# Landmark sums of two batches by DMA transfers that add, negated row maxima in tiles of their own, and a new order of work (Nyström attention, then a squared-ReLU MLP, one core)

## The chip, the cores and the metric

The kernel runs on one core of one Trainium2 chip. The metric is the device time in microseconds (us) of one execution, as a median of several runs. One further execution was recorded by the hardware profiler; every duration below comes from its trace, and line numbers such as L486 are lines of the kernel before. In the changed file the same statements stand some 3 to 34 lines further down.

The engines are PE (TensorE, matrix products), DVE (VectorE), ACT (ScalarE), POOL (GpSimd) and SP (SyncE). Each works through its own instructions in program order and waits at an instruction whose inputs are not there. Loads are issued by POOL, stores by SP (the very last one by ACT too).

## The reference, cut to what matters

```
q, k, v: (8 batches, 8 heads, 576 tokens, 64) float32;   m = 32 landmarks, 18 tokens each
q_lm = mean of q over each run of 18 tokens;   k_lm likewise
A  = softmax(q  k_lm^T / 8)        (576 x 32)
Bm = softmax(q_lm k_lm^T / 8)      (32 x 32)
C  = softmax(q_lm k^T / 8)         (32 x 576)
Z  = Bm^T / (norm1(Bm) * norminf(Bm) + 1e-6);   6 times: Z = 2 Z - Z Bm Z
x  = A Z C v, heads side by side:  (4608 tokens, 512)
out = relu(x w_in)^2 w_out,        w_in 512 x 2048, w_out 2048 x 512
```

## The kernel before

All work is cut into named steps, some 1400 of them. Batch b (0 to 7) is one round of `attention(b)`, `ffn1(b)` and pieces of `ffn2`. A table `ORDER` lists the steps in one line of words; the position of a word sets the order in which its engine meets it, and a suffix (`/A`, `/D`, `/P`, `@bank`) sets the engine or the PSUM bank. So the order on every engine's queue is written out by hand (or by a search); a small planner only checks it against its own costs and fills gaps of the first 30 us with idle products on `onesb` (L1198).

The steps that matter here:

- `ldq`, `ldk`, `ldv` (L425, L441): POOL issues the load of q, k or v of half a batch, float32 in memory to bfloat16 on the chip. 288 KB arrive per transfer of q or k; for v there are transfers of 288, 216 and 72 KB.
- `lx` (L431) and `lm` (L486), batches 3 to 7: `lx` loads q and k of the batch a second time, laid out by runs of tokens in the tile `XS` (96 partitions); `lm` sums the 18 tokens of each landmark with 48 products on PE, and `lme` (L414 or L418) copies the scaled sums from PSUM into `LM`. `lmt` transposes them (L544), and `B`, `SS` (L560, L743, L748) need the result. Batches 0 to 2 sum with the identity in other forms (L501, L508).
- `N`, `U`, `bd`: the six iterations for Z. `bd` (L649) spreads a 32 x 32 block to a diagonal tile `BD`, on POOL or on DVE; the product `N` on PE (L712) needs it; `U` (L726, DVE) makes the next iterate.
- `Amx`, `Aex`, `Asu`, `Arc`, `Aml` of batches 0 and 1: the softmax of A. In batch 0, cut in four parts (`BY_ROW`), `Amx` (L973, DVE) writes the negated row maxima into the tile `smA`, and `Aex` (L978) is one ACT instruction per row with that maximum as its bias.
- `CV` (L834), `ZC`, `W` (L905, into PSUM, copied to `WP` by `We`), `F` (L1077, the first MLP product, into PSUM), `R` and `Q` (ReLU and square on ACT or DVE), `O` (L1124, the second MLP product; one step is four products of a 128-token tile), `Oe` and `St` (copy and store of a 128-token tile, 256 KB).

Of the kernel before, what the change touches and what calls it, by code (L numbers as in the profile page):

```python
# [264 lines left out]
def kernel(  # L265
# [32 lines left out]
    XS = mk("XS", [96, 2, H, 6, D], BF16)  # L298
# [21 lines left out]
    smA = [mk(f"smA{u}", [P, 3, 2, n], F32) for u, n in enumerate(A_LEN)]  # L320
    w_in = mk("w_in", [P, 4, D_FF], BF16)
# [106 lines left out]
    def load_xs(b):  # L428
        for t in range(2):
            src = (q, k)[t][b].rearrange("h (p j) d -> p h (j d)", j=6)  # L430
            op(f"lx{b}.{t}", {"POOL": 0.8}, lambda e, t=t, src=src: nc.gpsimd.dma_start(  # L431
                XS[:, t].rearrange("p h j d -> p h (j d)"), src),
               W=[("XS", t)], nbytes=1179648, queue="sw")

# [25 lines left out]
    def attention(b):  # L460
# [17 lines left out]
        def landmarks_rows():  # L478
# [3 lines left out]
            def lmx(e):  # L482
                xs = XS[:].rearrange("p t (r c) j d -> p t r c j d", r=2)
                for j in range(6):
                    for c in range(4):
                        nc.tensor.matmul(view()[quad(c)], lhsT=seg[:], rhs=xs[:, :, :, c, j, :],  # L486
                                         start=(j == 0), stop=(j == 5))
# [450 lines left out]
        for u in range(2) if b in TOKENS else ():  # L938
# [28 lines left out]
            for j, (x0, x1) in enumerate(zip(cuts, cuts[1:])):  # L967
# [4 lines left out]
                op(f"Amx{b}.{u}{z}", {"DVE": v_(w)}, lambda e, s3=s3, p3_=p3_, pS=pS, at=at, neg=by_row:  # L972
                   nc.vector.tensor_reduce(s3(0)[:, at], p3_(pS)[:, at], axis=AX.X, op=ALU.max, negate=neg),  # L973
                   R=[pS], W=kx_("amx"))

                def rows(e, s3=s3, sa3=sa3, p3_=p3_, pS=pS, x0=x0, x1=x1):
                    for x in range(x0, x1):
                        nc.scalar.activation(sa3[:, x], p3_(pS)[:, x], AF.Exp, bias=s3(0)[:, x:x + 1])  # L978
# [8 lines left out]
                op(f"Asu{b}.{u}{z}", {"DVE": v_(w)}, lambda e, s3=s3, sa3=sa3, at=at: eng(e).tensor_reduce(  # L987
# [172 lines left out]
    def loads(what, b):  # L1160
# [53 lines left out]
ROWS = (3, 4, 5, 6, 7)  # L1214
# [14 lines left out]
ROW = 0.12  # L1229
# [31 lines left out]
R1.4 St2 F1.12@5 R1.0 N2.3@2 Q1.4 lm3.0@7 U2.3 R1.12 Q1.0 bd2.4/D F1.8@2 lme3.0 Q1.12 lx4.0
N2.4@5 F1.14@0 lmt3.0 R1.8 U2.4 ldk5.1 Q1.2 B3@6 R1.14 F1.20@4 Bmx3 Bsb3 T3.01 ldv2.00 Bex3 R1.20
SS2.0@0,2,6 Bsu3 At2.0 Q1.20/A ldv3.10 SS2.1@4 Q1.14/A bd2.5 Cmx2.0 O5.0@6 lx4.1 Cmx2.1 Cex2.0
O5.1 At2.1 Cex2.1 F1.22@0 Brc3 Amx2.0 Bml3/P F1.10@4 ldq6.1 R1.22 Btf3 F1.28@2 Crc2.1 Asb2.0
R1.10 O4.0@7 ldk4.0 Q1.22 R1.28 ldv3.11 Amx2.1 N2.5@5 F1.16@0 Btr3/A Q1.8/A Bcs3 U2.5 F1.18@2
Zm2.0 R1.16 Zm2.1 Bct3 F1.30@4 Zm2.3 Bnm3 Aex2.0 bt3/D O4.1 Q1.10 Asb2.1 R1.18 O4.2 ldv4.11
Cnr2.1 R1.30 Bad3 Brn3 Asu2.0 Q1.18/A Zi3/P F1.24@2 F1.26@4 T3.00 Aex2.1 O4.3 Q1.16 R1.26 ldq6.0
CT2.1 R1.24 BBT3@0 O5.2 Yi3 Arc2.0 Asu2.1 bd3.0 Q1.24/A O5.3 ldq5.0 Oe4.0 Aml2.0 ldv3.00 Q1.26/A
SS3.0@2,4,0 St4 O7.0@7 Q1.28/A At3.0 Oe5.0 O7.1 Ab2.0 St5 Crc2.0 Arc2.1 Cnr2.0/A Aml2.1 SS3.1@0
O6.0@6 Q1.30/A Cmx3.1 O6.1 At3.1 Cex3.1 CT2.0 O7.2 Cmx3.0 Amx3.0 CV2@4,0 Cex3.0 Crc3.1 Zm2.2 O7.3  # L1270
CVe2.0/A CVe2.1 ldv5.11 T4.11 ldv5.00 ZC2@3 N3.0@5 O6.2 Asb3.0 ZCe2.0 ldk6.0 ZCe2.1 ldv4.00 U3.0
W2.1@2 Aex3.0 Amx3.1 W2.2@0 W2.0@4 bd3.1 Oe7.0 Ab2.1 O6.3 We2.0/D We2.1 St7 O8.0@7 We2.2 Crc3.0
# [6 lines left out]
lm5.0@5 Q2.9/A Zm3.0 CV3@2,0 Btf4 R2.13 Zm3.2 Q2.12 O9.1 Btr4/A lme5.0/D CVe3.0/A ldv6.10 Zm3.1
Q2.14/A Arc3.1 Aml3.1 lx6.1 O10.0@5 CVe3.1/A Ab3.1 lx6.0 ZC3@6 O10.1 lmt5.0 ZCe3.0 Bcs4 Ab3.0  # L1280
ZCe3.1 ldv5.10 Q2.13/A Bct4 B5@2 W3.0@6 bt4 Bnm4 Q2.15/A Bmx5 W3.1@0 Bad4 Bsb5 O10.2 ldk5.0
We3.1/D Bex5 We3.0 O10.3 Bsu5 Brc5 T4.00 BBT4@6 F3.0@0 Bml5/P Oe10.0 ldv6.00 F3.1@2 Btf5 Brn4
R3.0 St10 Zi4 O9.2 Yi4 R3.1 bd4.0/D T4.10 N4.0@7 Q3.1/A W3.3@5 U4.0 W3.2@0 F3.2@2 We3.3 bd4.1
We3.2/D O12.0@7 R3.2 Q3.0 F3.5@5 Btr5/A Q3.2 N4.1@2 F3.6@0 T5.00 R3.5 O9.3 R3.6 Bcs5 Bct5 Q3.5
F3.7@5 Oe9.0 U4.1 F3.3@0 bd4.2/D St9 F3.4@2 R3.3 N4.2@4 O12.1 R3.4 U4.2 bd4.3/D Q3.6/A Bnm5
F3.10@0 T5.11 N4.3@4 Q3.3/A F3.9@2 U4.3 O12.2 bd4.4/D R3.9 R3.10/D R3.7 N4.4@4 O12.3 U4.4 bd4.5/D
Q3.9 F3.13@2 Oe12.0 Q3.10 N4.5@6 O11.0@5 Bad5 R3.13 bt5/D U4.5 Zm4.3 BBT5@0 Q3.13/A Brn5
SS4.0@1,3,6 Yi5 Q3.4/A bd5.0/D O11.1 Zi5 Zm4.0 Zm4.2 c7 At4.0 Q3.7/A N5.0@0 O11.2 Amx4.0 SS4.1@6
U5.0 O11.3 Cmx4.0 bd5.1 Cmx4.1 O13.0@0 Oe11.0 At4.1 Cex4.1 O13.1 St11 Cex4.0 N5.1@5 F3.11@6 U5.1
St12 Asb4.0 F3.8@3 R3.11 O14.0@5 R3.8/D Q3.11/A F3.14@6 Crc4.1 Aex4.0 Amx4.1 F3.12@1 Cnr4.1  # L1290
# [78 lines left out]
```

## Time and profile before

| | |
|---|---|
| median of 3 runs | 261.68 us (261.16 to 262.84) |
| the profiled execution | 261.07 us, of which the span from first to last instruction is 259.4 us |
| PE busy | 249.6 us, 96% of the span |
| DVE, ACT, POOL busy | 210.0, 181.1, 67.9 us |
| idle products on PE (L1198) | 44, in the first 30 us |
| read from memory, written | 48.50 MB, 9.44 MB |

An engine's busy time is an average over very different stages. What matters is, stage by stage, which engine never rests and what it waited for when it did.

### The profile page before, as it was taken

The numbers are of one execution on the slowest core, as the hardware profiler recorded it, in microseconds if no ns is written. First come the engines' busy times: TensorE is split into PE (matmuls) and PEld (weight loads), VectorE is DVE, ScalarE is ACT, GpSimd is POOL, SyncE is SP. The second block draws the span as 40 slices with busy tenths as digits, with TensorE's granted clock in tenths as the row PEclk, the third lists the DMA queues.
The fourth block names the chain that finished last, engine by engine and source line by source line (L and its number), as shares of the span: only waits on it lengthen the run. The fifth ranks groups of instructions, "written<-read, shape, count | busy, mean of one in ns | idle before, by whom it ended". The sixth has DMA issues, their size and how long they took to land.

```text
span 259.4 us, 7586 instructions
## 1 busy us (share of the span) xinstructions
PE 249.6 (96%) x3094; PEld 139.6 (54%) x3094; DVE 210.0 (81%) x547; ACT 181.1 (70%) x362; POOL 67.9 (26%) x117
## 2 busy tenths in 40 slices
PE   7987999999999998999999999999999999999993
PEld 2555565556554566465454556466454575457542
DVE  3678997788999999897999789989899999757321
ACT  4576797578998889788687498886693994367300
POOL 8555827434731540620231411000002000000000
PEclk9999999999999999999999999999999999999999
DMA  6999999999999999794259595051103050033034
GB/s 107 203 189 204 205 212 206 208 238 230 223 208 222 223 217 226 108 211 118 48 95 167 103 204 104 4 124 40 43 3 81 3 123 3 3 87 77 13 91 101
DMA packets 25123, 34.18 MB, mean 132 GB/s; under 512 B 2432, under 2 KB 14464, under 8 KB 25088
## 3 DMA queue, kind: packets, MB, share of 16 engines
q0 software_dynamic: 19168, 24.25, 55.2%
q1 hardware_dynamic: 5760, 9.31, 13.9%
q8 instruction: 24, 0.39, 0.6%
q10 hardware_dynamic: 160, 0.13, 0.2%
q14 instruction: 11, 0.09, 0.1%
HBM read 48.50 MB, written 9.44 MB: 223 GB/s over the span
## 4 chain that ended last, share of the span: by engine, by line
PE 73%; DMA 12%; POOL 5%; issue 4%; ACT 3%; DVE 1%; POOLq 0%
PE ps L1124 42%; PE ps L1077 19%; DMA XS<-in_k_dram 9%; DMA X<-in_q_dram 3%; PE ps L905 3%; ACT SA L978 2%; PE ps L834 2%; POOL X L425 1%; PE ps L486 1%; PE ps L748 1%; POOL V L441 1%; PE ps L1003 1%; POOL BD L649 1%; PE ps L1198 1%; PE ps L712 1%
## 5 line engine op out<-in xcount | busy, mean ns | idle before, releaser
L1124 PE MATMUL ps<-w_out,G 128*128 128x512 bf16 (+1 forms) x592 | 138.0, 374 | 0.0
L1124 PEld LDWEIGHTS <-G 128*128 128x128 bf16 x592 | 54.2, 98 | 54.4 <-issue 5.7
L1098 ACT ACTIVATE RS<-ps 128x576 bf16<-128x576 f32 (+2 forms) x106 | 64.9, 652 | 14.2 <-PE ps L1077 7.0
L1077 PE MATMUL ps<-AT,WP 128*128 128x288 bf16 (+2 forms) x512 | 72.2, 286 | 0.1
L1077 PEld LDWEIGHTS <-WP 128*128 128x128 bf16 x512 | 47.9, 98 | 20.0 <-issue 2.9
L1105 ACT ACTIVATE G<-RS 128x576 bf16<-128x576 bf16 (+2 forms) x50 | 33.5, 687 | 1.7 <-DVE RS L1100 1.2
L1107 DVE TENSOR_TENSOR G<-RS 128x576 bf16<-128x576 bf16 (+2 forms) x76 | 32.4, 447 | 2.2 <-ACT RS L1098 1.6
L412 ACT COPY OS<-ps 128x512 f32<-128x512 f32 (+1 forms) x31 | 17.7, 572 | 21.7 <-PE ps L1124 20.9
L649 POOL TENSOR_TENSOR BD<-ST,blkb 128x256 bf16<-128x256 bf16 x13 | 9.8, 751 | 61.1 <-DVE ST L726 61.0
L412 ACT CAST WP<-ps 128x1024 bf16<-128x1024 f32 (+1 forms) x23 | 21.6, 981 | 3.9 <-PE ps L905 3.7
L470 DVE STREAM_TRANSPOSE TT<-X 128x576 uint32<-128x576 uint32 x32 | 23.8, 758 | 0.1
L789 ACT ACTIVATE C<-ps,sm 128x576 bf16<-128x576 f32 x16 | 14.2, 904 | 10.7 <-DVE sm L786 10.6
L441 POOL DMA_DIRECT2D V<-in_v_dram x24 | 12.8, 534 | 30.6 <-PE ps L834 22.8
L1100 DVE TENSOR_SCALAR RS<-ps 128x576 bf16<-128x576 f32 (+2 forms) x22 | 16.4, 752 | 4.5 <-PE ps L1077 3.8
L726 DVE SCALAR_TENSOR_TENSOR ST<-ST,ps 128x128 bf16<-128x128 bf16 (+1 forms) x48 | 12.6, 263 | 5.2 <-PE ps L712 2.0
L1198 PE MATMUL ps<-onesb 128*128 128x512 bf16 (+1 forms) x41 | 12.5, 413 | 1.6 <-DVE onesb L348 1.6
L416 DVE CAST WP<-ps 128x1024 bf16<-128x1024 f32 (+1 forms) x11 | 12.3, 1114 | 0.9 <-PE ps L905 0.7
L786 DVE TENSOR_REDUCE sm<-ps 128x1 f32<-128x576 f32 x16 | 11.5, 742 | 0.9 <-PE ps L748 0.9
L416 DVE COPY OS<-ps 128x512 f32<-128x512 f32 x6 | 4.1, 688 | 10.1 <-PE ps L1124 10.0
L1030 DVE STREAM_TRANSPOSE SA<-ps 128x320 f32<-128x320 f32 (+1 forms) x24 | 10.0, 455 | 0.5 <-PE ps L743 0.5
L905 PE MATMUL ps<-w_in,ZC 64*32 64x512 bf16 x256 | 10.2, 382 | 0.0
L425 POOL DMA_DIRECT2D X<-in_k_dram x16 | 9.3, 582 | 2.5 <-DMA w_out<-in_moe_w_out_dram 1.0
(142 smaller groups left out, 291.6 us busy)
## 6 DMA issues: line engine op xcount, KB each, us to landing
out_dram<-OS SPq DMA_DIRECT2D x70, 128.0 KB, 2.4
X<-in_k_dram POOLq DMA_DIRECT2D x16, 288.0 KB, 9.3
X<-in_q_dram POOLq DMA_DIRECT2D x16, 288.0 KB, 11.4
XS<-in_q_dram POOLq DMA_DIRECT2D x5, 576.0 KB, 9.0
XS<-in_k_dram POOLq DMA_DIRECT2D x5, 576.0 KB, 12.1
V<-in_v_dram POOLq DMA_DIRECT2D x8, 288.0 KB, 9.4
w_in<-in_moe_w_in_dram POOLq DMA_DIRECT2D x8, 256.0 KB, 10.4
w_out<-in_moe_w_out_dram POOLq DMA_DIRECT2D x4, 512.0 KB, 11.1
```

Of the source, the lines that this page charges most:

```text
L412: nc.scalar.copy(o, i)
L416: eng(e).tensor_copy(o, i)
L441: lambda e, r=r, p0=p0, n=n, src=src: nc.gpsimd.dma_start(vv[32 * p0:32 * (p0 + n), r].rearrange("p s d -> p (s d)"), src),
L470: op(f"T{b}.{t}{r}", {"DVE": v_(576) + 0.02}, lambda e, r=r: nc.vector.transpose(tt[:, t, r].rearrange("p s m e -> p (s m e)").bitcast(U32 ...
L905: nc.tensor.matmul(ps[quad(pos_a(c, r)), pW.at + r, :], lhsT=zcs[r][half, pos_c(c, r), :], rhs=w_in[half, c, 512 * ch:512 * ch + 512], sta ...
L1077: nc.tensor.matmul(ps[:, ph.at + i, 0:w], lhsT=wp[:, r, 128 * ff:128 * ff + 128], rhs=at[:, r, t0:t0 + w], start=(r == 0), stop=(r == 1))
L1098: nc.scalar.activation(rs, pair(ph, w), AF.Relu)
L1100: nc.vector.tensor_scalar(out=rs, in0=pair(ph, w), scalar1=0.0, scalar2=None, op0=ALU.max)
L1105: nc.scalar.activation(g, rs, AF.Square)
L1107: eng(e).tensor_tensor(g, rs, rs, ALU.mult)
L1124: nc.tensor.matmul(bank(po)[:, 0:c1 - c0], lhsT=G[:, f, lo:lo + P], rhs=w_out[:, f, c0:c1], start=(f == 0), stop=(f == NF - 1))
L1198: nc.tensor.matmul(ps[:, j, 0:w], lhsT=onesb[:, 0:P], rhs=x[:, 0:w], start=True, stop=True)
```

## The change

Three things change.

First, batches 6 and 7 no longer use `lx` and `lm`. Instead `load_sums` has POOL issue 18 transfers per batch (`la`), nine for q and nine for k. Each brings two of the 18 tokens of every landmark: 128 partitions, each with 2 runs of 128 float32 numbers, 128 KB. The first of nine writes, the other eight add to what lies there, so each must wait until the one before it has landed; POOL does the waiting. The sums lie as float32 in the space of `XS` (batch 6 in its q half, batch 7 in its k half). What is left are two places per landmark, which `lmc` (ACT) and `lme` (DVE) scale and add into `LM`. PE has no part in it.

Second, in batch 0 the negated maxima of the four parts go to four small tiles `NM` instead of `smA`.

Third, `ORDER` is new throughout, and the planner's cost of a row of `Aex` is 0.19 instead of 0.12. Among other things the warm-up `c7` and some copies change place or engine: `lme1.0`, `CRe0` and `Bmb0` go from ACT to DVE.

```diff
-    XS = mk("XS", [96, 2, H, 6, D], BF16)
+    XS = mk("XS", [P, 2, H, 6, D], BF16)
+    ACC = [XS[:, i].rearrange("p h j d -> p (h j d)")[:, 0:16 * D].bitcast(F32)
+           .rearrange("p (t r s d) -> p t r s d", t=2, r=2, s=2) for i in range(2)]
...
+    NM = {k: mk("NM" + "".join(map(str, k[1:])), [P, 10], F32) for k in BY_ROW}
...
+    def load_sums(b):
+        for j in range(SEG // 2):
+            for t in range(2):
+                src = (q, k)[t][b].rearrange("(r c) (m s) d -> (c m) r (s d)", r=2, s=SEG)
+                op(f"la{b}.{t}{j}", {"POOL": 0.57}, lambda e, j=j, t=t, src=src: nc.gpsimd.dma_start(
+                    ACC[b % 2][:, t].rearrange("p r s d -> p r (s d)"), src[:, :, 2 * D * j:2 * D * (j + 1)],
+                    accum_op=ALU.add if j else ALU.bypass),
+                   R=[("ACC", b % 2, t)] if j else [], W=[("ACC", b % 2, t), *([] if j else [("XS", b % 2)])],
+                   nbytes=ADD_COST * 262144, queue="sw")
...
+        def landmarks_added():
+            acc, ls, kS = ACC[i2], LS[:, 0, 0:256].rearrange("p (t r d) -> p t r d", t=2, d=D), ("LS", 0)
+            R = [("ACC", i2, t) for t in range(2)]
+            op(f"lmc{b}.00", {"ACT": a_(256), "DVE": v_(256)}, lambda e: copy(e, ls, acc[:, :, :, 1], scale=LMS),
+               R=R, W=[(kS, 0), (kS, 1), (kS, "w")])
+            op(f"lme{b}.0", {"DVE": v_(256)}, lambda e: nc.vector.scalar_tensor_tensor(
+                out=lm[:], in0=acc[:, :, :, 0], scalar=LMS, in1=ls, op0=ALU.mult, op1=ALU.add),
+               R=[*R, (kS, 0), (kS, 1)], W=[("LM", i2, r) for r in range(2)], port=("DVE",))
...
-            if b in ROWS:
+            if b in ADDED:
+                landmarks_added()
+            elif b in ROWS:
...
-                   nc.vector.tensor_reduce(s3(0)[:, at], p3_(pS)[:, at], axis=AX.X, op=ALU.max, negate=neg),
+                   nc.vector.tensor_reduce(s3(0)[:, at] if neg is None else neg[:, 0:at.stop - at.start],
+                                           p3_(pS)[:, at], axis=AX.X, op=ALU.max, negate=neg is not None),
...
-                        nc.scalar.activation(sa3[:, x], p3_(pS)[:, x], AF.Exp, bias=s3(0)[:, x:x + 1])
+                        nc.scalar.activation(sa3[:, x], p3_(pS)[:, x], AF.Exp, bias=nm[:, x - x0:x - x0 + 1])
...
-ROWS = (3, 4, 5, 6, 7)
+ROWS = (3, 4, 5)
+ADDED = (6, 7)
+ADD_COST = 1.5
...
-ROW = 0.12
+ROW = 0.19
...
-Asu0.1a N0.1@7 Crc0 Arc0.1a lm1.0a Cmk0 U0.1 Aml0.1a/P Amx0.0a Asu0.1b N0.2@0 Aex0.0a lm1.0b
...
+lm1.0@0 U0.0 CT0.0 Aex0.1a N0.1@2 Asu0.1b lm1.0a U0.1 win31 T1.01 N0.2@3 lm1.0b U0.2 Amx0.0b
```

The new order at three places. Each row is an instruction, with its line, what it writes and reads, and the shape.

DVE in batch 0, from the first row maxima of A to the second iterate of Z (`SCALAR_TENSOR_TENSOR ST`), before:

```order
L973 TENSOR_REDUCE smA_119<-ps 128x10
L636 TENSOR_REDUCE sm_117<-ps 128x2
L643 RECIPROCAL sm_117<-sm_117 128x2
L673 TENSOR_TENSOR ST_0_96<-ps,sm_117 128x2x32
L670 TENSOR_TENSOR ST_0_96<-Bf_104,sm_117 128x2x32
L795 STREAM_TRANSPOSE CT<-C_83 128x9x32
L973 TENSOR_REDUCE smA_119<-ps 128x10
L726 SCALAR_TENSOR_TENSOR ST_1_97<-ST_0_96,ps 128x128
L987 TENSOR_REDUCE smA_119<-SA_76 128x10
```

and now:

```order
L997 TENSOR_REDUCE NM1b<-ps 128x10
L660 TENSOR_REDUCE sm_117<-ps 128x2
L667 RECIPROCAL sm_117<-sm_117 128x2
L819 STREAM_TRANSPOSE CT<-C_84 128x9x32
L697 TENSOR_TENSOR ST_0_96<-ps,sm_117 128x2x32
L835 RECIPROCAL sm_117<-sm_117 128x2
L997 TENSOR_REDUCE NM1a<-ps 128x10
L997 TENSOR_REDUCE NM0a<-ps 128x8
L750 SCALAR_TENSOR_TENSOR ST_1_97<-ST_0_96,ps 128x128
```

Three of the four row maxima now stand ahead of the first `U`, each in a tile of its own; the multiplication that makes the first Z has gone to POOL.

POOL in batch 5's iterations for Z, ahead of where batch 6's landmarks are needed. Before (the `BD` rows are `bd5.1`, `bd5.2` and `bd5.4`; `bd5.0` and `bd5.3` were DVE's):

```order
L649 TENSOR_TENSOR BD_101<-ST_1_99,blkb 128x256
L649 TENSOR_TENSOR BD_100<-ST_0_98,blkb 128x256
L441 DMA V_65<-in_v_dram 32x1152
L425 DMA X_62<-in_k_dram 128x1152
L441 DMA V_66<-in_v_dram 96x1152
L441 DMA V_66<-in_v_dram 128x1152
L425 DMA X_63<-in_k_dram 128x1152
L649 TENSOR_TENSOR BD_100<-ST_0_98,blkb 128x256
L431 DMA XS<-in_q_dram 96x8x384
L431 DMA XS<-in_k_dram 96x8x384
```

and now (the `BD` rows are `bd5.0` to `bd5.2`, the rows of L442 the transfers that add):

```order
L673 TENSOR_TENSOR BD_100<-ST_0_98,blkb 128x256
L442 DMA XS<-in_k_dram 128x2x128
L442 DMA XS<-in_q_dram 128x2x128
L673 TENSOR_TENSOR BD_101<-ST_1_99,blkb 128x256
L442 DMA XS<-in_k_dram 128x2x128
L428 DMA X_62<-in_k_dram 128x1152
L454 DMA V_66<-in_v_dram 32x1152
L442 DMA XS<-in_k_dram 128x2x128
L442 DMA XS<-in_q_dram 128x2x128
L673 TENSOR_TENSOR BD_100<-ST_0_98,blkb 128x256
```

Between two `BD` steps, which PE waits for, POOL now meets one to three transfers, each of which first waits for the landing of its predecessor.

ACT where batch 6's landmarks are made (`LS<-XS` is `lmc6.00`), a place where the row did not exist before:

```order
L813 ACTIVATE C_83,sm_118<-ps,sm_118 128x2x288
L813 ACTIVATE C_84,sm_118<-ps,sm_118 128x2x288
L417 ACTIVATE LS<-XS 128x256
L1123 ACTIVATE RS_131<-ps 128x576
L1123 ACTIVATE RS_128<-ps 128x576
L1130 ACTIVATE G<-RS_128 128x576
```

The first ReLU of the next stretch of `F` (L1123) stands right behind it on ACT.

More of the change, by code (lines that the diff above doesn't have):

```diff
@@ L986, in attention @@
                         sa3[:, at], sa3[:, at], AF.Exp), R=kx_("sa"), W=kx_("sa"))
[L987 removed]
+                op(f"Asu{b}.{u}{z}", {"DVE": v_(w), **({"POOL": p_(w)} if (b, u, z) in POOL_S else {})}, lambda e, s3=s3, sa3=sa3, at=at: eng(e).tensor_reduce(
                     s3(1)[:, at], sa3[:, at], axis=AX.X, op=ALU.add), R=kx_("sa"), W=kx_("asu"), port=("POOL",))
@@ L1171, in loads @@
             load_xs(b)
+        elif what == "sums":
+            load_sums(b)
         elif what == "win":
@@ L1181 @@
     for b in range(B):
-        if b in ROWS:
+        if b in ADDED:
+            loads("sums", b)
+        elif b in ROWS:
             loads("xs", b)
@@ L1261 @@
[L1261 to L1272, printed above, removed]
@@ L1279 @@
[L1279 to L1290, printed above, removed]
@@ new lines @@
+bd4.1 F3.3@2 R3.2/D la7.02 O12.0@5 R3.3 Q3.2 Oe9.0 F3.6@6 T4.10 N4.1@0 O12.1 St9 R3.6 U4.1 la6.03
+bd4.2/D Q3.3/A Bnm5 F3.9@3 la7.11 Bad5 T4.01 St10 Q3.1/A F3.7@6 la6.12 N4.2@0 F3.5@1 Q3.6/A
+ldv4.11 R3.7/D O12.2 ldv6.11 R3.5 U4.2 Q3.0/A F3.4@6 Q3.5 O12.3 R3.9/D bd4.3 R3.4 la7.03 F3.13@0
+Q3.9 Oe12.0 N4.3@2 la6.04 F3.10@3 R3.13 U4.3 O11.0@6 la7.12 bd4.4/D R3.10 Q3.4 Q3.7 la6.13 Btr5/A
+N4.4@2 O11.1 Q3.13/A U4.4 ldk7.0 T5.10 SS4.0@4,2,0 bd4.5/D O11.2 At4.0 N4.5@7 O11.3 Brn5 U4.5 bt5
+Amx4.0 SS4.1@0 la7.04 Oe11.0 O13.0@7 la6.05 Cmx4.1 Q3.10/A St11 Zi5/P At4.1 O15.0@6 Cex4.1 la6.14
@@ new lines @@
+Zm4.3 St12 Asb4.0 O15.1 ldv5.10 Cmx4.0 la7.13 Aex4.0 BBT5@2 F3.8@0 ldq7.0 Zm4.2 O13.1 Cex4.0 Yi5
+Amx4.1 bd5.0 Asu4.0 F3.14@2 R3.8 F3.11@4 Zm4.1 R3.14 Arc4.0 O14.0@1 Crc4.0 Aml4.0 R3.11 Q3.8/A
+F3.12@2 la6.15 Q3.11 O14.1 Q3.14 la6.06 R3.12 Cnr4.0 CT4.0 F3.15@4 Crc4.1 N5.0@0 Cnr4.1 O13.2
+R3.15 Zm4.0 U5.0 Q3.12 O15.2 Q3.15/A CT4.1 Asb4.1 CV4@2,4 Ab4.0 Aex4.1 bd5.1 O15.3 CVe4.1/A
+CVe4.0 la6.16 Asu4.1 ZC4@5 ldk6.0 O13.3 ZCe4.0 Arc4.1 ldv7.11 Aml4.1 ZCe4.1 Oe15.0 N5.1@0 O14.2
+la7.14 Oe13.0 Ab4.1 St15 la6.07 U5.1 W4.0@2 W4.2@6 bd5.2 W4.3@4 We4.0 O16.0@0 ldv5.00 We4.3/D
```

167 lines of the change are left out of this document (91 added, 76 removed).

## The prediction

> **What bounds the kernel now.** I read the totals first, then the kernel cut into stages, then what PE waited for, then the transfers. Totals, then the windows (busy us per engine, instruction counts in brackets, granted clock, mean busy share of the 16 DMA engines, GB/s):
>
> ```profile
> PE 249.6 (96%) x3094; PEld 139.6 (54%) x3094; DVE 210.0 (81%) x547; ACT 181.1 (70%) x362; POOL 67.9 (26%) x117
> 0.00:30.40 30.40, 26.34 (x418) 14.41 (x418) 20.83 (x70) 18.09 (x70) 20.17 (x41) 1.00 1.05 180
> 30.40:104.00 73.60, 71.90 (x980) 41.72 (x972) 66.28 (x174) 61.33 (x112) 29.72 (x49) 1.00 1.16 218
> 104.00:156.00 52.00, 52.00 (x680) 28.48 (x677) 45.77 (x121) 40.05 (x76) 14.68 (x24) 1.00 0.75 133
> 156.00:241.40 85.40, 85.40 (x963) 47.80 (x962) 74.32 (x181) 59.54 (x104) 3.37 (x5) 1.00 0.23 52
> ```
>
> From 104 us on PE never rests and its clock is full; between 30 and 104 us it lacks 1.7 us. There time is gained only by giving PE less to do, or by ending a wait. In the first 30.4 us PE's 26 us are largely filler: those products (L1198) wait for nothing and compute nothing. What sets that stage is the chain through ACT and DVE to the first `F` (L1077 starts at 30.41). The DMA engines are full until about 104 us (share 1.05 to 1.16; queues overlap, so 1 is no ceiling), then not.
>
> The waits of PE, and of DVE and ACT around the row maxima:
>
> ```profile
> L486 PE MATMUL ps<-XS,seg 96*32 96x256 bf16 x120 | 4.2, 274 | 0.7 <-DMA XS<-in_k_dram 0.7
> L717 PE MATMUL ps<-ST 32*32 32x64 bf16 (+1 forms) x96 | 2.8, 190 | 2.0 <-DVE ST L726 1.9
> 17.39 0.49 DVE L973 TENSOR_REDUCE smA<-ps 128x10 f32<-128x320 f32 x1 [0.89 <-ACT SA L978]
> 17.80 0.28 DVE L726 SCALAR_TENSOR_TENSOR ST<-ST,ps 128x128 bf16<-128x128 bf16 x1
> 21.26 0.42 DVE L973 TENSOR_REDUCE smA<-ps 128x8 f32<-128x256 f32 x1 [0.74 <-ACT SA L978]
> 15.48 1.88 ACT L978 ACTIVATE SA<-ps,smA 128x32 f32<-128x32 f32 x10
> 17.92 3.31 ACT L978 ACTIVATE SA<-ps,smA 128x32 f32<-128x32 f32 x18 [0.56 <-DVE smA L973]
> 20.98 0.52 ACT L414 ACTIVATE LM<-ps 128x256 bf16<-128x256 f32 x1
> 21.72 1.53 ACT L978 ACTIVATE SA<-ps,smA 128x32 f32<-128x32 f32 x8 [0.22 <-DVE smA L973]
> ```
>
> Each engine waits for the other over one tile: DVE's next maxima (L973) wait until ACT has read the last ones, and ACT's next rows wait for DVE. Behind DVE's first such wait stands the first `U` (L726), and PE's iterations (L717) wait for `U`.
>
> **The sums leave PE (-1.54).** Batch 6's `lm`, in the chain of waits and in the timeline:
>
> ```profile
> 145.01 0.77 PE ps L486 x24
> 144.94 0.84 PE L486 MATMUL ps<-XS,seg 96*32 96x256 bf16 x24
> ```
>
> 0.77 us of PE's time, in a stage where PE is the bound, twice (batches 6 and 7): 1.54 us. The copy `lme` that follows it on DVE becomes one copy on ACT and one combination on DVE, each of 256 columns; the like took 0.52 us (L414 above) and there is room: ACT is busy 40 of 52 us in that stage.
>
> **The maxima in their own tiles, and the prologue's order (-1.0).** DVE's two waits for ACT are 0.89 + 0.74 = 1.63 us, ACT's for DVE 0.56 + 0.22 = 0.78, and `lme1.0` (0.52, between ACT's rows) goes to DVE. On DVE the work stays and the waits go, so the first `F` could start up to 1.63 us earlier, or not at all, if the loads of w_in or a step further on hold it. The DMA engines are full there (share 1.05). I take 1.0, bounds 0 and 1.6. The planner's 0.19 per row costs nothing on the chip.
>
> **Batch 5's load (-0.7).** PE's wait of 0.73 us at 103.20 was for the second `XS` load of batch 5:
>
> ```profile
> 91.89 11.27 DMA XS<-in_k_dram
> 103.20 0.84 PE L486 MATMUL ps<-XS,seg 96*32 96x256 bf16 x24 [0.73 <-DMA XS<-in_k_dram]
> ```
>
> In the new order `lx5` stands after the same PE work, but of the loads just ahead of it three (`ldk6.0`, `ldv5.00`, `ldv4.00`, 288 KB each) have moved behind it, and one (`ldk5.1`) has come in. Two fewer at 218 GB/s are 2.7 us of queue. I count the wait as gone, bounds 0 and 0.73.
>
> **The adding transfers (+0.3, and the risk).** No row shows one. What they do to POOL, the queue and the engines comes from the nearest rows: the loads in the lightly loaded stretch (KB written, us from issue to landing), and what issuing one costs POOL:
>
> ```profile
> XS<-in_q_dram POOLq DMA_DIRECT2D x1, 576.0 KB, 6.0
> V<-in_v_dram POOLq DMA_DIRECT2D x1, 216.0 KB, 3.5
> L441 POOL DMA_DIRECT2D V<-in_v_dram x24 | 12.8, 534 | 30.6 <-PE ps L834 22.8 <-DMA XS<-in_q_dram 2.1 <-DMA w_out<-in_moe_w_out_dram 1.8
> L449 POOL DMA_DIRECT2D w_in<-in_moe_w_in_dram x8 | 5.0, 632 | 3.3 <-DMA X<-in_q_dram 2.3 <-DMA X<-in_k_dram 0.8
> L431 POOL DMA_DIRECT2D XS<-in_q_dram x5 | 4.1, 823 | 7.4 <-PE ps L486 7.4
> L649 POOL TENSOR_TENSOR BD<-ST,blkb 128x256 bf16<-128x256 bf16 x13 | 9.8, 751 | 61.1 <-DVE ST L726 61.0
> ```
>
> Without their issue they took 5.2 and 3.0 us: 360 KB more in 2.2 us, or 164 KB written (327 KB float32 read) per us, and a fixed 3.0 - 216/164 = 1.7 us. One adding transfer reads 128 KB and, if the old sum is read too, 128 KB more: 0.39 or 0.78 us by bytes. By runs: `XS` is 768 runs in 576/164 = 3.5 us, 4.6 ns each; 256 runs are 1.2 us, and 2.3 if each is fetched twice. Bounds 0.4 and 2.3; I take 1.0, between the two middle ones. Issue: 256 runs like w_in's, 0.63. So one link of a chain takes 0.63 + 1.7 + 1.0 = 3.3 us in an empty queue.
>
> *The chain.* Between `la6.10` and `la6.18`, eight links, the new order has 28 `O` and 21 `F` steps and smaller ones on PE; with these two lengths
>
> ```profile
> 155.22 0.98 PE ps L1077 x8
> 156.20 0.86 PE ps L1124 x4
> ```
>
> (an `F` is 4 products, 0.49) that is 28 x 0.86 + 21 x 0.49 = 34 us, some 40 with the rest: 5.0 per link. From the issue of `la6.18` to `lmc6.00` there are three `O` and an `F` and one score step, some 3.5 us. 3.3 fits, barely.
>
> *The engines.* In 104 to 156 us the share was 0.75. The four `XS` loads of batches 6 and 7 leave it (4 x 3.5 = 14 us, 0.27), 31 of the 36 adds come before `lmc6.00` (31 us, 0.60): 0.75 - 0.27 + 0.60 = 1.08, under the 1.16 of the full stretch. The point from which the queue falls behind is (1.16 - 0.48) x 52 / 31 = 1.14 us per transfer.
>
> *POOL.* In that stretch POOL gets some 25 issues more, 16 us on top of 14.7 of 52; but most now wait for a landing, and behind them stand eight `BD` steps of batches 4 and 5 and `bt5`, for which PE's products wait in order. A `BD` takes 0.75 and comes, at its tightest (`bd4.3`, `bd5.3`), half an `O` ahead of its product. I take 0.3 us for these, bounds 0 and 3.
>
> The Trainium skill ("DMA: Bandwidth & Descriptors", section "Anatomy of one DMA") fits a transfer on this path as 2.0 us plus bytes over 436 GB/s. An estimate by it for 128 KiB is 2.3 us, of which 0.3 load the engines; the share would be about 0.66, and no lateness possible. For the 216 KB row it gives 2.5 where the trace has 3.0 after issue, and the 576 KB row 3.4 for 5.2, so I stay with the rows.
>
> **The sum.** 261.07 - 1.54 - 1.0 - 0.7 + 0.3 = 258.1 against the profiled execution (span 259.4 and 1.7 around it). That execution lies 0.6 under the median of the runs and below all three, so I add 0.4: 258.5 us, 1.2% under 261.68. Its own range is 256.8 (all gains in full) to 260.5.
>
> **Rivals.** *The adds are slow.* An adding transfer that reads and writes back takes 1.5 us (half more than I took; the bound by runs is 2.3). Then the share wanted is 0.48 + 31 x 1.5/52 = 1.37, 1.18 times what the engines gave: 52 us of loads take 9.4 us longer. `lmc6.00` waits in order on ACT with the ReLUs behind it, PE has two `F` and an `O` ahead of it (1.8 us) and then stands: 258.5 + 7.6 = 266. For it: an add is a read, a read and a write, and no run shows its price. Against: the fetch by bytes is 0.8. It decides from 1.14 us on.
>
> *POOL passes the waits on.* The queue keeps up, but each of the nine `BD` steps comes 0.3 us later to a PE that waits in order: +2.7, 261.2. For it: `BD` stands right behind a transfer at most of these places. Against: spacing 5.0 for links of 3.3.
>
> *The waits in the prologue move instead of going.* Full DMA engines until 104 us and DVE busy 66 of 73.6 suggest that what ACT no longer holds, loads or DVE do: only PE's 1.54 is left: 261.07 - 1.54 + 0.3 + 0.4 = 260.2.
>
> **How the numbers follow.** Forecast 0.54, slow adds 0.32, POOL 0.08, prologue 0.06. A measurement of this kernel can tell about 1% from no change, 2.6 us. Of the forecast's 0.54 I put 0.46 below 259.06 and 0.08 above; the last two rivals lie within 1%; the first lies over it. So faster 0.46, within 1% 0.22, slower 0.32. The range: from 256.5, all gains and a little of the small waits on PE, up to 266.5, which takes in slow adds of up to 1.5 us and leaves out the dearer ones.
>
> **What would show it.** Right: no L486 after 104 us; DVE's maxima without a wait for ACT, and the first `F` near 29.4; no wait of PE at batch 5's `lm`; the adds' landings about 3 to 4 us after issue; ACT's `LS<-XS` without a wait; share near 1.1 at 104 to 156. Wrong: landings of 5 us and more, ACT idle ahead of `LS<-XS` until a DMA, PE idle after an `N` that waits for POOL's `BD`, or a first `F` at 30.4 again.

## The result and the profile after

The change is slower: 271.3 us median (270.5 to 274.0) against 261.56 us (here of four runs), ratio 1.038, 95% interval 1.032 to 1.044. A second session with the same two kernels gave 270.53 against 260.85, ratio 1.037 (1.033 to 1.040). The forecast was 258.5 us, and its range ended at 266.5.

The totals of the change's profiled execution (span 269.7 us, 271.4 with what lies around it), and the same windows as in the prediction: us, busy time per engine (PE, PEld, DVE, ACT, POOL) with instruction counts, granted clock, DMA share, GB/s.

```profile
PE 251.6 (93%) x3041; PEld 139.4 (52%) x3041; DVE 214.3 (79%) x551; ACT 179.8 (67%) x352; POOL 113.8 (42%) x157
```

```profile
0.00:30.40 30.40, 25.62 (x397) 14.22 (x397) 20.11 (x71) 16.11 (x65) 20.36 (x40) 0.94 1.03 174
30.40:104.00 73.60, 71.99 (x956) 42.09 (x956) 65.98 (x171) 59.77 (x107) 32.20 (x51) 1.00 1.15 214
104.00:156.00 52.00, 44.90 (x550) 23.01 (x548) 39.26 (x98) 36.47 (x65) 43.84 (x48) 0.99 0.91 148
```

In the third window PE was busy for all of 52.00 us before. Now it lacks 7.1 us there, while POOL went from 14.68 to 43.84 us, 29 us more where the prediction had counted 16. The DMA share is 0.91 in the mean, not the 1.08 that was feared. So POOL is where to look first; its costliest groups on the page (busy us, mean ns of one, idle before), the wait of PE, and the adding transfers' landings:

```profile
L442 POOL DMA_DIRECT2D XS<-in_q_dram x18 | 29.7, 1842 | 13.1 <-PE ps L499 8.0
L442 POOL DMA_DIRECT2D XS<-in_k_dram x18 | 29.9, 1928 | 7.0 <-DMA XS<-in_k_dram 6.2
L673 POOL TENSOR_TENSOR BD<-ST,blkb 128x256 bf16<-128x256 bf16 x15 | 18.5, 1234 | 27.4 <-DVE ST L750 22.2
L736 PE MATMUL ps<-ST,BD 128*128 128x64 bf16 (+1 forms) x72 | 8.0, 193 | 6.3 <-POOL BD L673 6.0
XS<-in_q_dram POOLq DMA_DIRECT2D x18, 128.0 KB, 5.2
XS<-in_k_dram POOLq DMA_DIRECT2D x18, 128.0 KB, 5.0
```

An adding transfer stands on POOL for 1.8 to 1.9 us (some of it queueing, for records overlap), against the 0.63 of the sum. `BD`, at 0.75 us each before, is listed at 1.23; its records overlap with the issues ahead of them in the same way, and one `BD` alone takes 0.70 (next fence). PE's `N` products (L736) wait for it; in this stage PE waited for nothing before. The largest of these waits in the chain of work that ended last:

```profile
145.66 7.83 DMA XS<-in_q_dram
153.50 0.02 issue
153.52 0.02 POOLq L442
153.54 0.49 issue
154.03 1.18 POOL XS L442
155.20 0.70 POOL BD L673
155.91 0.05 issue
155.96 0.29 PE ps L736 x2
```

```profile
155.96 0.29 PE L736 MATMUL ps<-ST,BD 128*128 128x64 bf16 x2 [3.87 <-POOL BD L673]
```

Read it downwards. A link issued at 145.66 lands at 153.50, 7.83 us later. POOL, which works in order, then issues the next link (1.18 us), and only then does the `BD` behind it (0.70). The product stands at the head of PE's queue meanwhile, and PE is idle for 3.87 us (second fence, the timeline).

Why did the landing take 7.83 us? The windows of 4 us around this wait, columns as above:

```profile
148.00:152.00 4.00, 3.34 (x22) 1.93 (x22) 2.15 (x4) 2.13 (x5) 4.00 (x5) 1.00 1.16 195
152.00:156.00 4.00, 0.14 (x2) 0.05 (x2) 0.00 (x0) 2.25 (x4) 2.02 (x3) 0.93 1.22 223
156.00:160.00 4.00, 4.00 (x74) 1.39 (x74) 2.85 (x5) 0.58 (x1) 2.94 (x4) 0.64 0.62 91
```

The shares of 1.16 and 1.22 are those of the full stretch before 104 us. So the mean of 0.91 hides moments in which the DMA engines were full, and a link has two parts: its issue on POOL and its landing. The pause has a second price. In the 4 us after it PE is busy throughout, but at a granted clock of 0.64; that is an estimated 4 x (1 - 0.64) = 1.4 us more.

How much is it? When ACT read the sums of batches 6 and 7, without a wait of its own:

```profile
L417 ACT ACTIVATE LS<-XS x2: 407/428/450, 163.2 to 181.8; 128x256 f32<-128x256 f32 x2
```

Between the start of batch 5's sums on PE (`lm5`) and ACT's read of batch 6's sums there are 58.9 us in the change (104.24 to 163.2). With the same transfers, not adding (first experiment), there are 50.0 (101.89 to 151.9). From that read to PE's last product it is 101.9 and 101.8 us. The 8.9 us of the adds lie in this stretch and nowhere else (8.5 us in the change's second execution).

The start went wrong too in this execution, in another way. The first sums on PE and the first `F`, of this execution and of the same kernel in the second session:

```profile
8.45 0.83 PE L530 MATMUL ps<-X,ident 64*64 64x128 bf16 x29 [1.79 <-DMA X<-in_q_dram]
31.43 1.47 PE L1102 MATMUL ps<-AT,WP 128*128 128x256 bf16 x12
```

```profile
7.13 0.70 PE L530 MATMUL ps<-X,ident 64*64 64x128 bf16 x36 [0.24 <-DMA X<-in_q_dram]
28.64 1.47 PE L1102 MATMUL ps<-AT,WP 128*128 128x256 bf16 x12
```

### The profile page after: what moved, and what is told of

It is laid out like the page before. It is cut to its first block, busy times and chain, and to the rows that moved or that the text cites. A ratio compares the mean times of both kernels' runs of the same rounds, so it can differ in the third digit from the quotient of the medians.

```text
span 269.7 us, 7547 instructions
## 1 busy us (share of the span) xinstructions
PE 251.6 (93%) x3041; PEld 139.4 (52%) x3041; DVE 214.3 (79%) x551; ACT 179.8 (67%) x352; POOL 113.8 (42%) x157
## 4 chain that ended last, share of the span: by engine, by line
PE 62%; POOL 11%; DVE 10%; DMA 7%; issue 4%; ACT 2%; SPq 1%; POOLq 0%
PE ps L1149 33%; PE ps L1102 17%; POOL XS L442 7%; DMA XS<-in_q_dram 3%; PE ps L929 3%; DMA X<-in_q_dram 2%; POOL BD L673 2%; PE ps L1227 2%; PE ps L858 2%; PE ps L772 1%; DMA XS<-in_k_dram 1%; DVE G L1132 1%; SPq L1162 1%; POOL V L454 1%; DVE TT L483 1%
## 5 line engine op out<-in xcount | busy, mean ns | idle before, releaser
L1123 ACT ACTIVATE RS<-ps 128x576 bf16<-128x576 f32 (+2 forms) x99 | 61.1, 650 | 11.4 <-PE ps L1102 7.0
L1130 ACT ACTIVATE G<-RS 128x576 bf16<-128x576 bf16 (+2 forms) x57 | 37.6, 683 | 6.8 <-DVE RS L1125 6.4
L442 POOL DMA_DIRECT2D XS<-in_q_dram x18 | 29.7, 1842 | 13.1 <-PE ps L499 8.0
L442 POOL DMA_DIRECT2D XS<-in_k_dram x18 | 29.9, 1928 | 7.0 <-DMA XS<-in_k_dram 6.2
L673 POOL TENSOR_TENSOR BD<-ST,blkb 128x256 bf16<-128x256 bf16 x15 | 18.5, 1234 | 27.4 <-DVE ST L750 22.2
L454 POOL DMA_DIRECT2D V<-in_v_dram x24 | 22.5, 1021 | 11.7 <-PE ps L858 6.6
L1125 DVE TENSOR_SCALAR RS<-ps 128x576 bf16<-128x576 f32 (+2 forms) x29 | 21.9, 757 | 6.8 <-PE ps L1102 4.3
L428 POOL DMA_DIRECT2D X<-in_q_dram x16 | 12.0, 752 | 5.4 <-DVE C L421 2.6
L736 PE MATMUL ps<-ST,BD 128*128 128x64 bf16 (+1 forms) x72 | 8.0, 193 | 6.3 <-POOL BD L673 6.0
L428 POOL DMA_DIRECT2D X<-in_k_dram x16 | 12.3, 767 | 2.5 <-DMA X<-in_k_dram 0.9
```

The source lines that it names most:

```text
L428: lambda e: nc.gpsimd.dma_start(x[:, t, r].rearrange("p s d -> p (s d)"), src),
L442: op(f"la{b}.{t}{j}", {"POOL": 0.57}, lambda e, j=j, t=t, src=src: nc.gpsimd.dma_start(ACC[b % 2][:, t].rearrange("p r s d -> p r (s d)"), ...
L454: lambda e, r=r, p0=p0, n=n, src=src: nc.gpsimd.dma_start(vv[32 * p0:32 * (p0 + n), r].rearrange("p s d -> p (s d)"), src),
L673: bdiag = lambda e, o, i: eng(e).tensor_tensor(o.rearrange("p r (c m) -> p r c m", c=4), i.unsqueeze(2).to_broadcast([P, 2, 4, M]), blkb[: ...
L1123: nc.scalar.activation(rs, pair(ph, w), AF.Relu)
L1125: nc.vector.tensor_scalar(out=rs, in0=pair(ph, w), scalar1=0.0, scalar2=None, op0=ALU.max)
```

## The experiments

The landmarks, from one profiled execution each; medians from all runs, ratios to the kernel before in the same session. "Rest" is from the start of `lm5` to the end of PE's last product. PE does 1.54 us of sums more in the kernels without adds.

| kernel | median us | ratio to before (95%) | first F | lm5 | rest |
|---|---|---|---|---|---|
| before | 261.5 | 1 | 30.41 | 103.20 | 152.1 |
| the change | 271.3 | 1.038 (1.032 to 1.044) | 31.43 | 104.24 | 160.8 |
| the change, again | 270.53 | 1.037 (1.033 to 1.040) | 28.64 | 103.08 | 160.5 |
| all plain | 260.78 | 0.996 (0.993 to 1.000) | 29.09 | 101.89 | 151.8 |
| only issues on POOL | 267.56 | 1.020 (1.013 to 1.027) | 29.03 | 101.88 | 159.5 |
| no adds | 261.28 | 0.998 (0.995 to 1.001) | 28.80 | 103.04 | 153.6 |
| no adds, bd2.5 on DVE | 261.17 | 0.999 (0.997 to 1.002) | 28.93 | 102.47 | 153.2 |
| maxima alone | 261.66 | 1.000 (0.997 to 1.002) | 30.68 | 103.16 | 152.1 |
| adds of batch 6 | 263.06 | 1.007 (1.004 to 1.010) | 28.80 | 103.34 | 154.4 |
| three links | 265.40 | 1.012 (1.006 to 1.018) | 28.57 | 101.83 | 156.3 |
| three links, early | 265.75 | 1.016 (1.012 to 1.020) | 28.82 | 101.62 | 156.9 |
| three links, tree | 260.71 | 0.998 (0.995 to 1.000) | 28.89 | 102.04 | 152.2 |

**All plain.** The transfers overwrite.

```
-    accum_op=ALU.add if j else ALU.bypass),
+    accum_op=ALU.bypass),
```

> Every one of the 36 transfers overwrites; none adds (so the sums of batches 6 and 7 are left out: what lands last stands for them). Sizes, waits, order and every other step stay. Theory P (an adding transfer holds POOL about 1.2 us instead of the 0.63 us of the sum, and N products wait behind the BD steps that queue after it): the transfers at L442 fall from a mean of 1842 and 1928 ns to under 900, POOL's busy time from 104 to 160 us falls from 46.8 us to about 30, PE's idle time there falls from 7.1 us to under 2, and the time is 263.5 us (262 to 265). Rival D (the chain of landings is what is late, whatever the issue costs): landings stay at 5 us, POOL still waits for them, the time stays at 269 to 272.

260.78 us, under P's range. Its first `F` came 2.3 us earlier than in the change's first execution (29.09 against 31.43), which is about what P's 263.5 us was too high by. POOL's issues and the landings:

```profile
L442 POOL DMA_DIRECT2D XS<-in_q_dram x18 | 13.3, 741 | 13.2 <-PE ps L499 8.0
L442 POOL DMA_DIRECT2D XS<-in_k_dram x18 | 13.1, 732 | 8.3 <-DMA XS<-in_k_dram 7.9
XS<-in_q_dram POOLq DMA_DIRECT2D x18, 128.0 KB, 3.3
XS<-in_k_dram POOLq DMA_DIRECT2D x18, 128.0 KB, 3.7
```

Same number, order and chains of waits: what costs is that they add. It more than doubles the busy time of these records on POOL (13 to 30 us per group, part of it queueing) and lengthens the landing from 3.3 and 3.7 to 5.2 and 5.0. Both go at once in this run, so it can't say which counts for how much. POOL's busy time in the stage did not fall to 30 us as expected, but to 38 (104 to 160 us).

**Only issues on POOL.** `BD`, `B` and `Z` steps among the adds go to DVE.

```
-bd4.1 ... bd4.3 ... bt5 ... bd5.0 ... Bml4/P ... Zi5/P
+bd4.1/D ... bd4.3/D ... bt5/D ... bd5.0/D ... Bml4 ... Zi5
```

> The adds stay as they are; the twelve small computations that POOL does among them (bd4.1, bd4.3, bt5, bd5.0 to bd5.5, and Bml4, Bml5, Zi5) go to DVE. Theory P (the loss comes through BD steps that stand behind issues on POOL): the 14 us of waits of the N products for POOL's BD go, the adds stay at 1.8 us each at L442, PE's idle time from 104 to 160 us falls from 7.1 to about 2 us, time 265 us (263 to 267). Rival D (the sums land late for what reads them): the wait moves to ACT's copy of the sums or to PE's first product of batch 6, time 269 to 272.

267.56 us, between the two ranges: both hold in part. No `N` waits for POOL any more, but what was waited there is mostly waited at the end, by ACT for the sums:

```profile
ACT LS L417 <- DMA XS<-in_k_dram: 6.8, 1, 6.8
POOL XS L442 <- DMA XS<-in_k_dram: 12.9, 6, 2.7
POOL XS L442 <- DMA XS<-in_q_dram: 4.8, 3, 2.6
```

From `lm5` to the read of batch 6's sums it is 56.8 us (the change 58.9, all plain 50.0). So the waits of `N` for `BD` are mostly where the late chain shows first, not a loss of their own. From the issue of `la6.10` to that of `la6.18`, eight links, it is 48.6 us here, 48.1 in the change and 41.5 in all plain, where PE's work sets the pace.

POOL's own time does not explain the 48.6. POOL was busy for 35.1 us of them, less than all plain's 41.5, and for 12.2 us it waited for landings. So without `BD` on POOL the landings set the pace as well: 5.1 to 5.2 us in the median from issue to landing, one link after the other on a queue that works in order.

**What one adding transfer costs.** Pairs that write and then add, in a quiet stretch at the end of the kernel without adds, and three adds in a row.

```
+    op("pa0", ... nc.gpsimd.dma_start(place, tokens, accum_op=ALU.bypass))
+    op("pa1", ... nc.gpsimd.dma_start(place, next_tokens, accum_op=ALU.add))
...
```

> The kernel without adds, and after batch 7's first N product, where POOL and its queue are idle, 13 transfers of tokens into a buffer that nobody reads any more: each pair writes a place and then, some 5 us later, adds to it: 256 runs of 512 bytes, 128 of 1024, 256 of 1536, 256 of 256 bytes; at the end three adding transfers of 256 runs of 512 bytes back to back. Theory P: adding by itself costs POOL: 0.75 us for the plain transfer of 256 runs of 512 bytes and 1.2 us for the adding one, landed after 2.6 and 4.2 us, and the three in a row end 1.2 us apart. By runs: 128 runs cost about 0.6 of it, 1536 bytes a run no more than 512. Rival B (the price goes by bytes): 1536 bytes a run take 2 us and more of POOL. Rival Q (it was only queueing in the change): adding and plain ones both 0.75 us, landed after 2.6 us.

POOL's timeline, by the first issue of each group: plain with 256 runs of 512 bytes; then adding, with 256 of 512, 128 of 1024, 256 of 1536, 256 of 256, and the last two of the row:

```profile
204.92 0.77 POOL L461 DMA_DIRECT2D XS<-in_q_dram  x1
...
207.75 1.24 POOL L461 DMA_DIRECT2D XS<-in_q_dram  x1 [2.07 <-DMA XS<-in_q_dram]
213.22 0.87 POOL L461 DMA_DIRECT2D XS<-in_q_dram  x1 [3.62 <-DMA XS<-in_q_dram]
218.49 1.21 POOL L461 DMA_DIRECT2D XS<-in_q_dram  x1 [3.65 <-DMA XS<-in_q_dram]
224.21 1.20 POOL L461 DMA_DIRECT2D XS<-in_q_dram  x1 [3.75 <-DMA XS<-in_q_dram]
229.92 2.43 POOL L461 DMA_DIRECT2D XS<-in_q_dram  x2 [1.77 <-DMA XS<-in_q_dram]
```

P holds on POOL, and by runs: 1.20 to 1.24 us for 256 adding runs, whether of 256, 512 or 1536 bytes, and 0.87 for 128 (0.7 of it, where 0.6 was expected); two in a row end 1.2 us apart. Rivals B and Q are out. On the DMA engines they differ as well. The queue's packets, MB and share while the first plain and the first adding transfer moved (16 packets of each are the signals of its end, and three of the second are the next transfer's):

```profile
q0 software_dynamic: 48, 0.13, 29.9%
...
q0 software_dynamic: 275, 0.14, 77.7%
```

The plain transfer goes in 32 packets of 4096 bytes, the adding one in 256 of 512 at 66 ns, 16 to an engine: 1.06 us, the 1.0 of the sum. The adding one's last packet ended 3.3 us after its issue began, and it was reported landed at 3.6 (the plain one at 2.5). The prediction had 3.3, with 0.6 less of issue and more behind it. So in an empty queue the link was sized nearly right; on POOL it was not.

**Half of the adds.** Only batch 6 is summed by adds; batch 7's tokens are loaded and summed on PE.

```
-ROWS = (3, 4, 5)
-ADDED = (6, 7)
+ROWS = (3, 4, 5, 7)
+ADDED = (6,)
```

> Only batch 6's sums come by adding transfers (18 of them, 16 adding); batch 7's go back to a load into XS after batch 6's sums are read, and to PE. Theory P (the loss is POOL's queue running out of time: in the change a round of four links takes 4 x 1.23 = 4.9 us of POOL and some 1.3 us for the loads and BD steps between, 6.2 us a round, where PE needs the next one after 5.0): a round of two takes about 3.8 us, the nine are through some 40 us after batch 5's sums, ahead of their reader; no wait of ACT for them, N products wait for POOL under 1 us, time 261.2 - 0.8 of PE work = 260.5 us (259.8 to 261.8). Rival E (each adding transfer costs the same wherever it stands, so half of them cost half of the 9 us): 265 to 266.

271.23 us, and it says nothing of this: I had left batch 7's load free to go into the buffer before batch 6's sums were read, so ACT read batch 7's tokens in place of the sums and waited 6.1 us for them. With the load behind the read:

```
+    R = [...] + [("XS", t) for t in range(2)]
```

> The kernel with only batch 6's sums by adding transfers once more, with batch 7's load into XS made to wait until batch 6's sums are read from it; in the run before it went ahead of that read, and ACT waited 6.1 us for it. Theory P (the loss is POOL's queue running out of time, so it does not grow in proportion): with 16 adding transfers instead of 32 the last one lands 0 to 1 us behind its reader, N products wait under 2 us for POOL, time 261.2 - 0.8 of PE work + 1 = 261.4 us (260.3 to 262.8). Rival E (each adding transfer costs its share wherever it stands): 265 to 266.

263.06 us, 0.3 above P's range and 2 under E's. The rest is 154.4 us, against 152.8 for no adds less one batch's 0.77: half of the adds cost 1.6 us, all of them 8.5 to 8.8 (160.5 and 160.8 against 153.6 - 1.54). So the loss does not go in proportion. ACT did not wait for the sums. PE waited 0.9 us for `BD`, 0.6 for a transpose on DVE, and for little else.

**No adds, and the start.** The sums of batches 6 and 7 go back to PE, in the new order.

```
-la6.00 ... la7.18 ... lmc6.00 ... lmc7.00
+lx6.1 lx6.0 ... lm6.0@3 ... lx7.0 lx7.1 ... lm7.0@1
```

> The new order and the maxima in tiles of their own stay; the sums of batches 6 and 7 go back to PE and to two loads into XS, at the places where the added sums were read. Theory P (the adds cost the middle 8.5 us, the start of the new order lost 2.5 us, batch 5's wait is gone): 271.3 - 8.5 + 1.5 of PE work = 264.3 us (263 to 266). The sum of the forecast (start 1.0 us earlier, adds 0.3 us): 259.8 us. Rival O (the order, not the adds, makes the N products wait): 269 or more. The first sums on PE began at 8.45 us in the change and at 6.93 us before: if that wait belongs to the order it is here too, if it was one execution's, it is not.

261.28 us, between the two, and rival O is out. The first sums began at 7.10 us, so the wait of 1.79 us was one execution's. Repeating the change gave the same:

> The change once more, unaltered. In its first profiled execution the first sums on PE began at 8.45 us and the first F product at 31.43; in seven kernels with the same start these were 7.0 to 7.3 and 28.6 to 29.1 us. Theory C (one execution's late landing): 7.0 to 7.3 and 28.6 to 29.2 us here, the time 269.5 to 271. Rival (the change's own): 8.4 and 31.4 again, 271.3.

7.13, 28.64, and 270.53 us. All eleven other executions with this start had the first `F` at 28.6 to 29.1. Yet the 1.3 to 1.8 us gained there are not in the time. In the kernel without adds, windows at 60 to 72 us:

```profile
64.00:68.00 4.00, 1.99 (x36) 0.84 (x37) 3.88 (x10) 2.92 (x6) 2.49 (x5) 0.72 1.10 222
68.00:72.00 4.00, 4.00 (x23) 2.23 (x22) 1.83 (x6) 1.77 (x5) 2.08 (x4) 0.85 1.21 205
```

PE is idle for 2.0 us, 1.3 of them for `bd2.5`, which stands on POOL behind a load of `X` that waits 1.0 us for an earlier landing (share 1.10). The granted clock is 0.72 in this window and 0.85 in the next. Moved:

```
-bd2.5
+bd2.5/D
```

> The kernel without adds, with bd2.5 alone on DVE where it was on POOL. Theory (the new order gives back what its start gained where POOL's bd2.5 stands behind loads of X that wait for their queue: PE idle 2.0 us at 64 to 68 us, and the granted clock 0.72 and 0.85 after it): the wait is gone and the time is 260.0 us (259.3 to 260.8). Rival (the wait was one execution's): the time stays at 261.3.

That wait is gone, but the time stays, 261.17:

```profile
PE ps L499 <- DMA XS<-in_k_dram: 1.5, 1, 1.5
```

Now `lm5` waits 1.5 us for its load. Most of what the start gains is taken back before 104 us, where the DMA engines are full: apart from the change's first execution, `lm5` began at 101.6 to 103.3 us in these kernels, at 103.20 before. In the two kernels without adds the rest is also 1.1 and 1.4 us longer than before's, with the same sums on PE; what the new order loses there stays open. The tiles alone, in the order of before:

```
-    tensor_reduce(s3(0)[:, at], ..., negate=by_row)
+    tensor_reduce(neg[:, 0:n], ..., negate=True)
```

> The kernel before, in its own order, with one thing of the change: the negated maxima of A's first batch go into four tiles of their own. Theory M (DVE's next maxima had waited for ACT's reads of the shared tile, and this makes the first F product of the four kernels with the new start 1.3 to 1.8 us earlier than the 30.4 us of before): first F near 29.4 us here too, time 260.5 us. Rival S (the order of the start does it, not the tiles): first F at 30.2 to 30.5 us, time 261.5 us.

Rival S, if a little later than it said: first `F` at 30.68, 261.66 us. And DVE's waits for ACT are still there, now with the new tiles' names:

```profile
DVE NM1b L974 <- ACT SA L980: 0.9, 1, 0.9
DVE NM0b L974 <- ACT SA L980: 0.7, 1, 0.7
```

The shared tile was not what held DVE. What did, I did not settle. In the new order 0.4 us of such waits is left (`NM1a`), in the change and in its second execution. Whether that order would gain as much without the new tiles, no run shows.

**Fewer transfers.** Three of six tokens at each place; DVE sums the six that are left.

```
-for j in range(SEG // 2): ... src[:, :, 2 * D * j:2 * D * (j + 1)]
+for j in range(3): ... src[:, :, 6 * D * j:6 * D * (j + 1)]
+tensor_reduce(ls, acc.rearrange("p t r s d -> p t r d s"), axis=AX.X, op=ALU.add)
```

> The same bytes are added by three transfers of six tokens each at each of the four places (12 instead of 36, 256 runs of 1536 bytes each instead of 512), and DVE sums the six that are left (1536 elements, estimated at 1.6 us, twice) where it summed two. Theory P with a price by transfer or by run: 12 issues at 1.2 us, some 30 us of POOL less than in the change, the N products wait no more, time 263 us (261.5 to 264.5). Price by bytes: issues of 3 us and more, the waits stay, 268 to 272. Rival D (landings): a link now moves three times as much, lands later, but there are only two between the first and the last; no wait from it.

265.40 us, between the two ranges. No `N` waits for POOL's `BD`. Issued earlier, with `BD` on DVE:

> Three links of six tokens as in the kernel with twelve transfers, issued earlier (at the places that the first, third and fifth transfer of each place have in the change); BD, B and Z steps among them go from POOL to DVE, and so does bd2.5. Theory (both losses of the change are the queue on POOL: BD steps behind adding transfers, and sums that land late): the last sum lands some 10 us ahead of its reader, no N product waits for POOL after 104 us, time 261.3 - 1.5 of PE work - 1 for bd2.5 + up to 1 for the 6 us more that DVE has to do = 259.5 us (258.5 to 261). Rival V (DVE becomes what bounds that stage): N products wait for DVE's BD and the time is 262 or more.

265.75, far above the theory's range, with POOL idle for most of the time from 120 us on. DVE bounds the stage, as rival V said, but not through `BD`. DVE's reduction over a stride is what lies between the sums and batch 6's `B` product:

```profile
L509 DVE TENSOR_REDUCE LS<-XS x2: 2725/2744/2764, 151.9 to 173.1; 128x256 f32<-128x1536 f32 x2
PE ps L1102 <- DVE OS L419: 2.1, 1, 2.1
PE ps L584 <- DVE LT L568: 1.9, 1, 1.9
```

2.74 us, not the 1.6 estimated, and DVE's other work queues behind it. In its place one addition of contiguous halves, placed ahead:

```
-tensor_reduce(ls, acc ..., axis=AX.X)
+lma: tensor_tensor(six[0:3], six[0:3], six[3:6], ALU.add)
+lmc, lmd, lme: LMS * t2; + LMS * t1; + LMS * t0
```

> Twelve transfers of six tokens as in the kernel with the early links, BD, B and Z steps back on POOL but for bd2.5; the last six tokens are summed by one DVE addition of 768 elements placed ahead (estimated 0.9 us), a copy with scale on ACT and two DVE steps of 256. Theory (what was left of the loss with twelve transfers is DVE's strided reduction, 2.74 us each, between the sums and batch 6's and 7's B product): PE's idle time from 140 to 180 us goes from 4.4 to under 1 us and the time is 260.2 us (259 to 261.5). Rival (the adding transfers themselves still cost what was lost): 264 or more.

```profile
L510 DVE TENSOR_TENSOR XS<-XS x2: 932/940/948, 145.2 to 166.3; 128x768 f32<-128x768 f32 x2
104.00:156.00 52.00, 51.84 (x586) 27.33 (x585) 45.96 (x116) 40.10 (x72) 26.53 (x37) 1.00 0.94 189
```

260.71 us against 260.85, within the range. PE is busy again for 51.84 of 52 us, and the rest of 152.2 us is 0.4 above all plain's 151.8: more than that the adds no longer cost, by these two executions. The DMA share of 0.94 is higher than the change's 0.91, and the landings are longer (5.4 and 7.5 us in the median). So neither full engines nor long landings are enough for the loss. With three links POOL pays 12 issues in place of 36, and each chain waits for two landings in place of eight; this run takes both away, and does not tell them apart. It is 3.6% under the change, and from before its interval (0.995 to 1.000) does not tell it.

## Why the prediction was wrong, step by step

- **"The adding transfers (+0.3, and the risk)."** This term of the sum failed: it measured 8.5 to 8.9 us. Two steps under it had the cost wrong, the issue and the link, and a third the wait.
- **"Issue: 256 runs like w_in's, 0.63."** An adding transfer of 256 runs takes 1.20 to 1.24 us of POOL, a plain one 0.72 to 0.77. The row was near in runs and wrong in kind: w_in's loads do not add. "16 us on top of 14.7" became 34.9 us in all plain and 43.8 in the change.
- **"5.0 per link ... 3.3 fits, barely."** The spacing was right: 40 us were reckoned for the eight links, and all plain took 41.5. The link in an empty queue was nearly right too (3.6 us to landing). But it was an empty queue's link, set against the pace of a loaded one. There the landing took 5.0 to 5.2 us in the median and 7.83 at worst, and POOL issues four chains and the loads in order, so each wait for a landing holds up what stands behind. I had never asked what the four chains do to each other's links. How much of the loss is issue and how much is landing stays open: each run that removed one removed the other.
- **"I take 0.3 us for these, bounds 0 and 3."** PE's waits for POOL's `BD` came to 6.0 us, 3.9 of them at one step, because what stood ahead of it was a link that waited for a landing. Rival "POOL passes the waits on" had named the place, at 0.08 and +2.7 us. "Against: spacing 5.0 for links of 3.3" was the argument that fell. Two of the signs of being wrong came true: landings of 5 us, and PE idle after an `N` that waits for `BD`.
- **"The engines."** Taken at 1.0 us per transfer, measured 1.06, so the 1.14 us from which rival "slow adds" was to decide was not reached. In the mean the share was 0.91 where 1.08 was reckoned, but around the longest wait it was 1.16 to 1.22. What that rival foretold, sums late for ACT, showed once `BD` was off POOL (6.8 us), though with a cheaper transfer than it assumed; its 266 was too little by 5.
- **"The sums leave PE (-1.54)."** Holds: no L486 (now L499) after 105 us, and all plain, with no such sums, has a rest 1.8 us shorter than no adds.
- **"The maxima in their own tiles, and the prologue's order (-1.0)"** and **"Batch 5's load (-0.7)"**. The first `F` was 1.3 to 1.8 us earlier (but for the change's first execution), more than taken, yet the tiles alone gave none of it. "Each engine waits for the other over one tile" was a wrong reading: with tiles of their own the two waits stayed. The two gains can't simply be added, for the time up to `lm5` hardly moved: it began 0.1 us earlier in the change's second execution. All plain has all three gains and no price of adding, and is 0.7 us under before, where the sum had 3.2; no adds is 0.2 under, where it had 1.7.
- **"Its own range is 256.8 ... to 260.5."** This does not follow from the bounds given: all gains in full are 257.6, and without the two uncertain gains, with the upper bound of 3 us for the adds, it is 262.9. Both lie far under 271.3.
- **The estimate beside the sum.** The fit that the Trainium skill gives ("DMA: Bandwidth & Descriptors", section "Anatomy of one DMA") makes 2.3 us for 128 KiB, an estimate. The plain transfer in the quiet stretch landed 2.5 us after its issue began, near it; the adding one took 3.6. The same section of the Trainium skill calls descriptor generation small, with many descriptors before the cost shows. For adding transfers the trace differs: 128 runs took 0.87 us of POOL, 256 took 1.2.

## What to carry to other kernels

In these runs a transfer that adds was paid on the engine that issues it, by its runs, and it landed later than a plain one. Before a chain of them is put on a queue, size it for all chains and loads that share the queue, issue and landing both, and not by one link in an empty queue. On a queue that works in order, whatever stands behind a link inherits the wait for the link before it, so keep steps that PE needs off that queue (by itself this brought 267.56 in place of 271.3 us), or use few transfers with long runs. A gain at the start counts only if the next load-bound point moves with it.

## What was not expected of the hardware

- Run length did not matter for an adding transfer on POOL: 256 bytes a run cost 1.20 us, 1536 bytes 1.21. On POOL the bytes came free up to there: twelve transfers moved what 36 did. The landing was not free of them: 5.2 us for 1536 bytes a run, 3.6 for 512, in the quiet stretch.
- Issues on POOL overlap in the records: the last two adding transfers of the quiet row begin 0.75 us apart and end 1.2 apart, so a group's mean (1.84 us) is more than the cost of one (1.2).
- Behind two of the pauses of PE the granted clock was low: 0.72 in the window of the 2.0 us without work at 64 to 68 us and 0.85 in the next, 0.64 in the 4 us after the change's 3.87 us. There the pause itself is not all that it costs. It is not so behind every pause: in three links, early, PE stood still for 1.95 us before 155.47, and the clock stayed at 1.00 (152 to 160 us).
